# Expert slots in two halves: one weight tile converted in each half, the activation chain over two slots

## Chip, cores and metric

One core of a Trainium2 chip. The metric is the device time of one execution in microseconds (us); several executions are timed and their median is used, and one execution is recorded by the hardware profiler. Engines are named as in the profile: PE (TensorE, with its weight loads PEld), DVE (VectorE), ACT (ScalarE), POOL (GpSimd) and SP (the engine that issues most of the loads and stores).

## What is computed

A retention layer (linear attention with a decaying state), followed by two expert layers, all in float32. With B = 4, H = 8, S = 768, D = 64 there are 3072 tokens of width 512; each expert layer goes from 512 to 2048 and back.

```
state = gamma * state + k_t v_t^T          # per batch and head, t = 0 .. 767
y_t   = (1/sqrt(D)) * q_t state
x = y as 3072 x 512
x = (h - tanh(h)) @ w_out    with h = x @ w_in        # first expert layer
x = elu(h) @ w2_out          with h = x @ w2_in       # second expert layer
```

## The kernel before

**Tiling.** Tokens are worked on in six blocks of 512 (`NB` = 6). The retention is done in chunks of 128 positions: step s is chunk s // 4 of batch s % 4, so four steps make one block of tokens. The steps of block 0 (s = 0 to 3) are done at the start, the other twenty one at a time inside the expert layers, in the slots 1 to 20.

**Slots.** The expert layers run in two phases (`ph` 0 and 1, one for each layer), each over six blocks, each over 16 tiles `f` of 128 hidden units: 192 slots, numbered `n`. In slot n, PE makes `h` of this slot (`first_mm`, L267: twelve 128 x 512 matmuls) and adds the product of slot n - 2 into the four accumulators (`second_mm`, L334: twelve more; `SKEW` = 2). Weights and activations are each split into a high and a low part, and three products of the parts stand for one float32 product.

**Weights.** They arrive as 64-bit numbers. `convert_a` (ACT, L81), `convert_b` (three DVE instructions, L89, L93, L97) and `convert_c` (ACT, L109, the high part, and L112, the low part, on DVE or POOL) make a tile pair of one raw tile; the raw tile, the 32-bit tile `w32` and the result are in SBUF. In phase 0, block 0, two tiles are converted in a slot, in slots 0 to 12, after six at the start; the weights of phase 1 are converted in the last block of phase 0 and the first of phase 1, mostly one in a slot.

**Activation chain.** From `h` (in PSUM) ACT makes `u`, `v`, `t` and a mask `m`, and DVE runs four instructions: L293 (`v` and `u`, both in SBUF), L296 (`v` and `h`), L299 (`h` and `t`) and L300 (copies `h` into `v` where `m` says so, and is the last reader of `h`). There are two `h` buffers. One slot later `split_hi` (ACT, L276) and `split_lo` (L280, POOL in the blocks marked `busy`, DVE elsewhere) split `v` into `g`. In phase 1 the chain has two instructions (L313, L316).

**Retention in a slot.** PE makes the scores (L163) into PSUM, DVE masks them (L175, one instruction over 1024 columns), PE makes the output from the state (L202) and from the masked scores (L210) and the new state part (L189); DVE scales the output (`out_scale`, L221) and adds the state part (L244), and POOL multiplies the state by its decay (L245). POOL also scales the next step's `v` by `vtab` (L143), and in four slots of a block it makes the low part of the next block's x (L365).

**Order.** `manual_schedule` keeps the order in which the code is written, engine by engine. Each engine works through its queue in that order and waits where an operand or a buffer is not ready. In a slot of block 0 DVE's queue is: mask, two operations of `side` (both L89), scaling, state sum, and then `chain` and the rest of `side` in turn:

```
if s is not None:
    for op in side[:2]:
        op()
    side = side[2:]
    out_scale(s)
    state_add(s)
interleave(chain, side)
```

Of the kernel before, what the change touches and what calls it, by code (L numbers as in the profile page):

```python
# [36 lines left out]
def retention_moe_kernel(ctx: ExitStack, tc: tile.TileContext, dims, ins, out):  # L37
# [15 lines left out]
    stg = ctx.enter_context(tc.tile_pool(name="stg", bufs=4))  # L53
# [49 lines left out]
    def convert_c(job, engine):  # L103
# [5 lines left out]
        nc.scalar.activation(out=t[:, 0, :], in_=w, func=AF.Copy)  # L109

        def low():
            engine.tensor_tensor(  # L112
                out=t[:, 1, :], in0=w, in1=t[:, 0, :].bitcast(F32), op=ALU.subtract
            )

        if engine is nc.gpsimd:
            low()
            return []
        return [low]
# [16 lines left out]
    def load_v(s):  # L136
        v = v_t[s] = att.tile([P, TB], F32, tag="v", bufs=B, name=f"v{s}")
        nc.sync.dma_start(out=v, in_=ins["qkv"][s][:, 2, :])
# [12 lines left out]
    def att_psum(s):  # L151

        tag = ("a", "acc0", "acc1")[s % 3] if s < B else "a"
        return (ps_a if tag == "a" else ps_acc).tile([P, 2, TB], F32, tag=tag, name=f"ps{s}")

    def scores_pe(s):
        t = qk_t[s]
        ps = ps_t[s] = att_psum(s)
        sc = ps.rearrange("p j (a i) -> p j a i", a=NP)
        for p in range(NP):  # L160
            for j in range(2):
                r = slice(j * D, (j + 1) * D)
                nc.tensor.matmul(  # L163
                    out=sc[:, j, p, :],
                    lhsT=t[r, 1, p * P:(p + 1) * P],
                    rhs=t[r, 0, p * P:(p + 1) * P],
                    start=True, stop=True,
                )

    def scores_mask(s):  # L170
        if s < B:
            pt = tmp.tile([P, 2 * NP, P], F32, tag="g", bufs=G_BUFS, name=f"pt{s}")
        else:
            pt = att1.tile([P, 2 * NP, P], F32, tag="pt", name=f"pt{s}")
        nc.vector.tensor_tensor(  # L175
            out=pt,
            in0=ps_t[s].rearrange("p j (a i) -> p (j a) i", a=NP),
            in1=mask.to_broadcast([P, 2 * NP, P]),
            op=ALU.mult,
        )  # L180
        pt_t[s] = pt

    def states_mm(ds, s):
        v, kn = v_t.pop(s), kn_t.pop(s)
        for p in range(NP):
            for j in range(2):
                r = slice(j * D, (j + 1) * D)
                h = 2 * p + j
                nc.tensor.matmul(  # L189
                    out=ds[r, p, :], lhsT=kn[:, h * D:(h + 1) * D], rhs=v[:, h * D:(h + 1) * D],  # L190
                    start=True, stop=True,
                )

    def out_pe(s):
        t, v, pt = qk_t.pop(s), v_t[s], pt_t.pop(s)
        o = ps_t[s][:, 0, :].rearrange("p (a i) -> p a i", a=NP)
# [9 lines left out]
        for p in range(NP):  # L206
            for j in range(2):
                r = slice(j * D, (j + 1) * D)
                h = 2 * p + j
                nc.tensor.matmul(  # L210
                    out=o[r, p, :], lhsT=v[:, h * D:(h + 1) * D], rhs=pt[:, j * NP + p, :],
                    start=(b == 0), stop=True, skip_group_check=True,
                )
        if b and b < NCH - 1:
            states_mm(ps_t[s][:, 1, 0:NP * D].rearrange("p (a d) -> p a d", a=NP), s)

    def out_scale(s):

        xo = xo_t[s] = att.tile([P, NP, P], F32, tag="xo", bufs=3, name=f"xo{s}")
        o = ps_t[s][:, 0, :].rearrange("p (a i) -> p a i", a=NP)  # L220
        nc.vector.tensor_tensor(out=xo, in0=o, in1=qtab, op=ALU.mult)  # L221
# [17 lines left out]
    def state_add(s):  # L239
# [3 lines left out]
        ds = ps_t[s][:, 1, 0:NP * D].rearrange("p (a d) -> p a d", a=NP)  # L243
        nc.vector.tensor_tensor(out=st[:, c], in0=ds, in1=st[:, c], op=ALU.add)  # L244
# [4 lines left out]
    def first_states():  # L249
        ds = ps_a.tile([P, B, NP, D], F32, tag="a", name="ds")  # L250
        for c in range(B):
            states_mm(ds[:, c], c)
        for c in range(B):
            nc.vector.tensor_tensor(
                out=st[:, c], in0=ds[:, c], in1=gtab.to_broadcast([P, NP, D]), op=ALU.mult
            )
# [64 lines left out]
    def second_mm(m, f, n):  # L321
        g, w = g_t.pop(n), wts[m, f]
        if f == 0:
            for i in range(2):
                t = ps_acc.tile([P, 2, TB], F32, tag=f"acc{i}", name=f"acc{n}_{i}")
                acc[2 * i], acc[2 * i + 1] = t[:, 0, :], t[:, 1, :]
# [46 lines left out]
    with tc.manual_schedule():  # L373
# [9 lines left out]
        def interleave_into(dst, lists):  # L383
            while any(lists):
                for ops in lists:
                    if ops:
                        dst.append(ops.pop(0))

        def interleave(*lists):
            while any(lists):  # L390
                for ops in lists:
                    if ops:
                        ops.pop(0)()

# [4 lines left out]
        AHEAD = 6  # L399
# [6 lines left out]
        for s in range(B):  # L406
            load_qk(s, stage[:, s])
            load_v(s)
            fetch(*jobs0[s])
# [3 lines left out]
        for job in jobs0[B:AHEAD]:  # L413
            fetch(*job)
        load_qk(B, att.tile([P, 2, TB], F32, tag="qk", name=f"qk{B}"))
        for job in jobs0[AHEAD:AHEAD + 4]:
            fetch(*job)

        def conv(*ids):
            ops = []  # L420
            interleave_into(ops, [convert_b(jobs0[i]) for i in ids])
            for op in ops:
                op()

        def conv_low(*ids):
            for i in ids:
                for op in convert_c(jobs0[i], nc.vector if i % 2 else nc.gpsimd):
                    op()
# [3 lines left out]
        for s in range(2):  # L432
            scale_v(s, nc.gpsimd)
        warm(3)
# [6 lines left out]
        conv(0)  # L441
        out_scale(0)
        scores_pe(2)
        out_pe(1)
        for s in range(2, B):
            scale_v(s, nc.gpsimd)
        conv(1)
        out_split(0)
        scores_mask(2)
        out_scale(1)  # L450
        conv_low(0, 1)
        convert_a(jobs0[2])
        convert_a(jobs0[3])
        scores_pe(3)
        out_pe(2)
        conv(2)
        out_split(1)
        scores_mask(3)
        out_scale(2)
        conv(3)  # L460
        out_pe(3)
        conv_low(2, 3)
        convert_a(jobs0[4])
        convert_a(jobs0[5])
        out_split(2)
        out_scale(3)
        out_split(3)
        first_states()
        conv(4, 5)
        conv_low(4, 5)  # L470
# [3 lines left out]
        rest = jobs0[AHEAD:]  # L474
        for f in range(NF):
            todo[f] = rest[:2]
            rest = rest[2:]
        assert not rest
        base = (NB - 1) * NF
        for f in range(NF):  # L480
            todo[base + f + 2] = [(2, f)]
        for f in range(NF):
            todo.setdefault(base + (8 + 5 * f if f < 2 else NF + f - 1), []).append((3, f))
# [5 lines left out]
        prev_jobs = []  # L489
        for job in todo[0]:  # L490
            convert_a(job)
        prev_v = None

        def flush():
            if prev_v is not None:
                g_t[n - 1] = split_hi(prev_v, n - 1)
                if lo_engine is nc.gpsimd:
                    split_lo(g_t[n - 1], prev_v, nc.gpsimd)
# [9 lines left out]

        n = 0
        for ph in range(2):  # L510
            for b in range(NB):
                for f in range(NF):
                    first, last = b == 0, b == NB - 1
                    if ph == 0 and first:
                        for job in jobs0[AHEAD + 4 + 2 * f:AHEAD + 6 + 2 * f]:
                            fetch(*job)
                    jobs = todo.get(n, [])
# [3 lines left out]
                    s = step_of.get(n)  # L521
# [15 lines left out]
                    if s is not None:  # L537
                        for op in side[:2]:
                            op()
                        side = side[2:]  # L540
                        out_scale(s)
                        state_add(s)
                    interleave(chain, side)
                    for job in todo.get(n + 1, []):
                        convert_a(job)
                    prev_v = v
                    prev_jobs = jobs
# [3 lines left out]
                    second(SKEW)  # L551

# [8 lines left out]
                    if s is not None:  # L561
                        out_store(s)
# [7 lines left out]
        flush()  # L570
# [59 lines left out]
```

## Time and profile before

| | us |
|---|---|
| median of 3 runs | 1224.04 (1222.66 to 1224.7) |
| time of the profiled execution | 1222.74 |
| its span, first to last instruction | 1221.0 |
| PE busy | 1158.8 (95%) |
| DVE busy | 709.9 (58%) |
| ACT busy | 623.1 (51%) |
| POOL busy | 244.7 (20%) |

How to read it: the shares are means over stages that differ. In the 40 slices of the page DVE shows 6 to 8 tenths over the first eight slices and 9 from the 22nd to the 26th, while PE shows 9 in nearly all slices after the ninth. The granted clock is the share of full speed that TensorE was given; its mean over the run is 0.978.

### The profile page before, as it was taken

What the parts mean: (1) busy time and instruction counts of PE and PEld (TensorE: products, weight loads), DVE (VectorE), ACT (ScalarE), POOL (GpSimd) and SP (SyncE); (2) the same over time, 40 slices, a digit from 0 to 9 for tenths busy, and PEclk for the clock granted to TensorE, in tenths of its full rate; (3) what the DMA queues carried; (4) which work ended last, traced back from release to release, by engine and by line L of the source; (5) the groups of instructions that cost most, each with busy time, mean ns of one, the idle gap of its engine ahead of it and who ended that gap; (6) DMA issues with size and microseconds to landing.
All of it is one profiled execution on the core that took longest, in us unless ns stands there. A gap on an engine that the chain in (4) does not pass through costs nothing.

```text
span 1221.0 us, 15860 instructions
## 1 busy us (share of the span) xinstructions
PE 1158.8 (95%) x6030; PEld 950.1 (78%) x6030; DVE 709.9 (58%) x1004; ACT 623.1 (51%) x1089; POOL 244.7 (20%) x183
## 2 busy tenths in 40 slices
PE   5688889799999999999998999999999999999998
PEld 3576767578888888888887788888888888888886
DVE  6778886455655656556599999535334334343332
ACT  2344443225565565556677766544444544544443
POOL 2243543200001001001057557201001010010000
PEclk7889999999999999999999999999999999999999
DMA  9457554421010010010176410100100100100000
GB/s 360 158 184 227 190 161 130 130 64 32 1 61 9 1 61 9 1 61 10 66 217 200 141 59 9 60 2 9 61 10 1 61 9 1 61 9 1 35 1 35
DMA packets 41581, 88.40 MB, mean 72 GB/s; under 512 B 3872, under 2 KB 14240, under 8 KB 41504
## 3 DMA queue, kind: packets, MB, share of 16 engines
q1 hardware_dynamic: 40928, 87.05, 21.9%
q8 instruction: 47, 0.77, 0.3%
q10 hardware_dynamic: 576, 0.33, 0.1%
q14 instruction: 30, 0.25, 0.1%
HBM read 69.54 MB, written 17.83 MB: 72 GB/s over the span
## 4 chain that ended last, share of the span: by engine, by line
PE 75%; DVE 2%; issue 1%; ACT 1%; DMA 0%; SPq 0%; ACTq 0%; DVEq 0%
PE h L267 37%; PE acc L334 37%; DVE w L93 1%; DMA qk<-qkv 0%; DVE v L300 0%; DVE w L97 0%; DVE v L293 0%; PE ps L163 0%; DVE h L299 0%; PE ps L210 0%; PE ps L202 0%; DVE v L296 0%; ACT t L290 0%; ACT g L276 0%; DVE w L89 0%
## 5 line engine op out<-in xcount | busy, mean ns | idle before, releaser
L267 PE MATMUL h<-x,w 128*128 128x512 f32 x2304 | 558.8, 391 | 5.5 <-DVE v L300 5.5
L267 PEld LDWEIGHTS h<-x,w 128*128 128x128 f32 x2304 | 432.2, 188 | 98.6 <-DVE v L300 6.8
L334 PE MATMUL acc<-g,w 128*128 128x512 f32 x1152 | 280.3, 392 | 0.0
L334 PE MATMUL acc<-w,g 128*128 128x512 f32 x1152 | 276.7, 389 | 0.6 <-DVE g L280 0.6
L334 PEld LDWEIGHTS acc<-w,g 128*128 128x128 f32 x1152 | 216.1, 188 | 45.9 <-DVE g L280 1.0
L334 PEld LDWEIGHTS acc<-g,w 128*128 128x128 f32 x1152 | 215.6, 189 | 46.1 <-ACT g L276 0.7
L313 DVE SCALAR_TENSOR_TENSOR v<-v,t 128x512 f32<-128x512 f32 x96 | 77.1, 803 | 274.3 <-ACT t L311 274.1
L308 ACT ACTIVATE u<-h 128x512 f32<-128x512 f32 x96 | 57.5, 599 | 252.4 <-PE h L267 252.0
L365 POOL TENSOR_TENSOR x<-xin,x 128x512 fp32r<-128x512 f32 x44 | 60.2, 1368 | 617.8 <-ACT x L364 617.8
L287 ACT ACTIVATE u<-h 128x512 f32<-128x512 f32 x96 | 57.3, 597 | 208.0 <-issue 153.0
L293 DVE SCALAR_TENSOR_TENSOR v<-v,u 128x512 f32<-128x512 f32 x96 | 73.2, 762 | 134.9 <-ACT v L288 134.9
L280 DVE TENSOR_TENSOR g<-v,g 128x512 fp32r<-128x512 f32 x145 | 114.7, 791 | 21.2 <-ACT g L276 21.2
L276 ACT ACTIVATE g<-v 128x512 fp32r<-128x512 f32 x192 | 118.2, 616 | 11.9 <-DVE v L300 9.7
L280 POOL TENSOR_TENSOR g<-v,g 128x512 fp32r<-128x512 f32 x47 | 66.2, 1409 | 154.4 <-ACT g L276 91.7
L81 ACT ACTIVATE w<-raw 128x512 f32<-128x512 f32 x64 | 41.8, 662 | 85.1 <-DVE w L112 65.4
L112 POOL TENSOR_TENSOR w<-w,w 128x512 fp32r<-128x512 f32 x48 | 73.6, 1535 | 24.3 <-ACT w L109 24.3
L300 DVE COPY_PREDICATED v<-m,h 128x512 f32<-128x512 uint16 x96 | 70.6, 736 | 7.0
L288 ACT ACTIVATE v<-u,qa_b 128x512 f32<-128x512 f32 x96 | 69.5, 724 | 4.3
L291 ACT ACTIVATE m<-u,xs_b 128x512 bf16<-128x512 f32 x96 | 68.1, 710 | 0.0
L296 DVE SCALAR_TENSOR_TENSOR v<-v,h 128x512 f32<-128x512 f32 x96 | 65.3, 680 | 2.6 <-ACT t L290 1.9
L299 DVE TENSOR_TENSOR h<-h,t 128x512 f32<-128x512 f32 x96 | 66.2, 690 | 0.0
L316 DVE TENSOR_TENSOR v<-h,v 128x512 f32<-128x512 f32 x96 | 65.4, 681 | 0.0
(40 smaller groups left out, 742.5 us busy)
## 6 DMA issues: line engine op xcount, KB each, us to landing
raw<-w SPq DMA_DIRECT2D x64, 512.0 KB, 4.6
qk<-qkv SPq DMA_DIRECT2D x20, 512.0 KB, 6.2
v<-qkv SPq DMA_DIRECT2D x24, 256.0 KB, 5.7
x1d<-o SPq DMA_DIRECT2D x12, 512.0 KB, 3.2
xin<-x1d SPq DMA_DIRECT2D x24, 256.0 KB, 5.0
kn<-qkv SPq DMA_DIRECT2D x20, 256.0 KB, 6.1
x0d<-xo SPq DMA_DIRECT2D x20, 256.0 KB, 2.6
xin<-x0d SPq DMA_DIRECT2D x20, 256.0 KB, 4.3
```

The lines of the kernel that those rows point to most:

```text
L112: engine.tensor_tensor(out=t[:, 1, :], in0=w, in1=t[:, 0, :].bitcast(F32), op=ALU.subtract)
L267: nc.tensor.matmul(out=h, lhsT=w[:, a, c * P:(c + 1) * P], rhs=x[:, b, c, :], start=(i == 0), stop=(i == 3 * KC - 1),)
L276: nc.scalar.activation(out=t[:, 0, :], in_=g, func=AF.Copy)
L280: engine.tensor_tensor(out=t[:, 1, :], in0=g, in1=t[:, 0, :].bitcast(F32), op=ALU.subtract)
L288: nc.scalar.activation(out=v, in_=u, func=AF.Square, bias=qa_b)
L291: nc.scalar.activation(out=big, in_=u, func=AF.Relu, bias=xs_b)
L293: lambda: nc.vector.scalar_tensor_tensor(out=v, in0=v, scalar=QB, in1=u, op0=ALU.add, op1=ALU.mult),
L299: lambda: nc.vector.tensor_tensor(out=h, in0=h, in1=th, op=ALU.subtract),
L300: lambda: nc.vector.copy_predicated(out=v, mask=big.bitcast(U16), data=h),
L313: lambda: nc.vector.scalar_tensor_tensor(out=v, in0=v, scalar=1.0, in1=th, op0=ALU.add, op1=ALU.mult),
L316: lambda: nc.vector.tensor_tensor(out=v, in0=h, in1=v, op=ALU.max),
L334: nc.tensor.matmul(out=acc[e], lhsT=lhsT, rhs=rhs, start=(f == 0 and i == 0), stop=(f == NF - 1 and i == 2),)
```

## The change

- Block 0 converts one weight tile in each half of a slot. `convert_c` is cut in two (`convert_c` for the high part, `convert_d` for the low), and `weights(i, first)` issues for half i: the high part (ACT) and low part of half i - 1's tile, `convert_b` of half i's, `convert_a` of half i + 1's. In block 0 the low part of the first half's tile goes to DVE, that of the second half's to POOL. Four tiles instead of six are converted at the start (`AHEAD`), 28 in the slots 0 to 13. `w32` has five buffers instead of four.
- In `busy` blocks the chain is cut in the middle: two instructions (phase 1: one) in its own slot, the rest at the head of the next slot, in turn with the weight operations of its first half. `split_hi` and `split_lo` of slot n - 1 are issued together, ahead of slot n's chain.
- Masks, scaling and state sum: the mask is two instructions of 512 columns into two tiles; the scores, the output and the state part have PSUM tiles of one bank each (tags a0, a1, acc0 to acc3). The mask is at the head of the slot's first half, scaling and state sum at its end, before the second half.
- The states of block 0 (`first_states`) move into slot 0, behind `first_mm`; stores of the retention's output (`out_store`) are issued one slot later; `v` has three buffers and one more in another tile; the loads at the start come in another order.

```diff
+    def convert_c(job):
         m, f = job
-        w = w32.pop(job)
         del raw[job]
         t = wts[job] = wp.tile([P, 2, TB], F32R, tag=f"w{m % 2}_{f}", name=f"w{m}_{f}")
+        nc.scalar.activation(out=t[:, 0, :], in_=w32[job], func=AF.Copy)
+
+    def convert_d(job, engine):
+        t = wts[job]
+        engine.tensor_tensor(
+            out=t[:, 1, :], in0=w32.pop(job), in1=t[:, 0, :].bitcast(F32), op=ALU.subtract
+        )
...
+        for j in range(2):
+            nc.vector.tensor_tensor(
+                out=pt[j], in0=ps_t[s][j], in1=mask.to_broadcast([P, NP, P]), op=ALU.mult
+            )
...
+        def weights(i, first):
+            ops = []
+            if i - 1 in todo:
+                job = todo[i - 1]
+                convert_c(job)
+                if first and i % 2:
+                    ops.append(lambda: convert_d(job, nc.vector))
+                else:
+                    convert_d(job, nc.gpsimd)
+            if i in todo:
+                ops = convert_b(todo[i]) + ops
+            if i + 1 in todo:
+                convert_a(todo[i + 1])
+            return ops
...
                     h = first_mm(2 * ph, xhl[ph * NB + b], f, n)
+                    if n == 0:
+                        for g in ds:
+                            next(g)
+                    ops = weights(2 * n, early)
+                    while chain or ops:
+                        if chain:
+                            chain.pop(0)()
+                        if ops:
+                            ops.pop(0)()
                     if s is not None:
                         out_pe(s)
-                    v, chain = (act_elu if ph else act_tanhshrink)(h, n, flush)
-                    low = []
-                    for i, job in enumerate(prev_jobs):
-                        low += convert_c(job, nc.vector if first and not ph and i else nc.gpsimd)
-                    side = []
-                    interleave_into(side, [convert_b(j) for j in jobs])
-                    side += low
-                    if prev_v is not None and lo_engine is nc.vector:
-                        side.insert(0, lambda: split_lo(g_t[n - 1], prev_v, nc.vector))
-                    if s is not None:
-                        for op in side[:2]:
-                            op()
-                        side = side[2:]
                         out_scale(s)
                         state_add(s)
-                    interleave(chain, side)
-                    for job in todo.get(n + 1, []):
-                        convert_a(job)
+                    def flush():
+                        if prev_v is not None:
+                            g_t[n - 1] = split_hi(prev_v, n - 1)
+                            split_lo(g_t[n - 1], prev_v, lo_engine)
+                    v, chain = (act_elu if ph else act_tanhshrink)(h, n, flush)
+                    for op in weights(2 * n + 1, early):
+                        op()
+                    cut = len(chain) // 2 if busy else len(chain)
+                    for op in chain[:cut]:
+                        op()
+                    chain = chain[cut:]
                     prev_v = v
```

Three places in the order of the queues. First DVE in a slot of block 0 (slot 3): before, from behind the mask to the last instruction of the chain (`pt` is the masked scores, `xo` the scaled output, `w_0_7` and `w_1_5` the 32-bit tiles of the two weights, `v` and `h` the chain's).

```order
L89 TENSOR_SCALAR w_0_7_580<-w_0_7_580 128x512
L89 TENSOR_SCALAR w_1_5_582<-w_1_5_582 128x512
L221 TENSOR_TENSOR xo_676<-ps_610,qtab 128x512
L244 TENSOR_TENSOR st<-ps_610,st 128x256
L293 SCALAR_TENSOR_TENSOR v_660<-v_660,u_658 128x512
L93 SCALAR_TENSOR_TENSOR w_0_7_580<-raw_7_402,w_0_7_580 128x512
L296 SCALAR_TENSOR_TENSOR v_660<-v_660,h_3_621 128x512
L93 SCALAR_TENSOR_TENSOR w_1_5_582<-raw_5_404,w_1_5_582 128x512
L299 TENSOR_TENSOR h_3_621<-h_3_621,t_659 128x512
L97 SCALAR_TENSOR_TENSOR w_0_7_580<-raw_7_402,w_0_7_580 128x512
L300 COPY_PREDICATED v_660<-m_661,h_3_621 128x512
L97 SCALAR_TENSOR_TENSOR w_1_5_582<-raw_5_404,w_1_5_582 128x512
```

And after, in the same slot, from the scaling on to the first half of slot 4 (the lines have moved by two to four: L178 is the mask, L223 the scaling, L245 the state sum, L296 to L303 the chain). Ahead of these rows stand two mask halves, the chain's second pair of slot 2 and the three weight instructions of the first half.

```order
L223 TENSOR_TENSOR xo_679<-o_653,qtab 128x512
L245 TENSOR_TENSOR st<-ds_670,st 128x256
L89 TENSOR_SCALAR w_1_4_646<-w_1_4_646 128x512
L93 SCALAR_TENSOR_TENSOR w_1_4_646<-raw_4_316,w_1_4_646 128x512
L97 SCALAR_TENSOR_TENSOR w_1_4_646<-raw_4_316,w_1_4_646 128x512
L112 TENSOR_TENSOR w_6_694<-w_0_6_580,w_6_694 128x512
L296 SCALAR_TENSOR_TENSOR v_685<-v_685,u_683 128x512
L299 SCALAR_TENSOR_TENSOR v_685<-v_685,h_3_630 128x512
L178 TENSOR_TENSOR pt_0_738<-ps_0_728,mask 128x512
L178 TENSOR_TENSOR pt_1_739<-ps_1_729,mask 128x512
L302 TENSOR_TENSOR h_3_630<-h_3_630,t_684 128x512
L89 TENSOR_SCALAR w_0_7_696<-w_0_7_696 128x512
```

Behind the scaling and the state sum there were chain and weights in turn; now five instructions that read SBUF alone follow one another.

Second, POOL around the same slot, before: the low part of g, the low part of the weights, the state's decay, the next v, and the next low part of g.

```order
L280 TENSOR_TENSOR g_664<-v_551,g_664 128x512
L112 TENSOR_TENSOR w_6_669<-w_0_6_485,w_6_669 128x512
L245 TENSOR_TENSOR st<-st,gtab 128x256
L143 TENSOR_TENSOR v_705<-v_705,vtab 128x512
L280 TENSOR_TENSOR g_771<-v_660,g_771 128x512
```

And after (L246 is the decay, L283 the low part of g, L141 the scaling of v):

```order
L112 TENSOR_TENSOR w_3_643<-w_1_3_530,w_3_643 128x512
L246 TENSOR_TENSOR st<-st,gtab 128x256
L283 TENSOR_TENSOR g_689<-v_569,g_689 128x512
L141 TENSOR_TENSOR v_716<-v_716,vtab 128x512
L112 TENSOR_TENSOR w_4_755<-w_1_4_646,w_4_755 128x512
```

The decay, which waits for DVE's state sum, now stands ahead of the low part of g.

Third, DVE at the start (L231 is the low part of a quarter of x), before:

```order
L175 TENSOR_TENSOR pt_194<-ps_169,mask 128x1024
L175 TENSOR_TENSOR pt_204<-ps_183,mask 128x1024
L89 TENSOR_SCALAR w_0_0_192<-w_0_0_192 128x512
L93 SCALAR_TENSOR_TENSOR w_0_0_192<-raw_0_120,w_0_0_192 128x512
L97 SCALAR_TENSOR_TENSOR w_0_0_192<-raw_0_120,w_0_0_192 128x512
L221 TENSOR_TENSOR xo_211<-ps_169,qtab 128x512
L89 TENSOR_SCALAR w_0_1_206<-w_0_1_206 128x512
L93 SCALAR_TENSOR_TENSOR w_0_1_206<-raw_1_125,w_0_1_206 128x512
L97 SCALAR_TENSOR_TENSOR w_0_1_206<-raw_1_125,w_0_1_206 128x512
L231 TENSOR_TENSOR x_235<-xo_211,x_235 128x4x128
L175 TENSOR_TENSOR pt_238<-ps_213,mask 128x1024
```

And after (L233 is the low part of x):

```order
L178 TENSOR_TENSOR pt_209<-ps_0_185,mask 128x512
L178 TENSOR_TENSOR pt_209<-ps_1_186,mask 128x512
L223 TENSOR_TENSOR xo_233<-o_200,qtab 128x512
L89 TENSOR_SCALAR w_0_0_195<-w_0_0_195 128x512
L93 SCALAR_TENSOR_TENSOR w_0_0_195<-raw_0_123,w_0_0_195 128x512
L97 SCALAR_TENSOR_TENSOR w_0_0_195<-raw_0_123,w_0_0_195 128x512
L223 TENSOR_TENSOR xo_240<-o_224,qtab 128x512
L178 TENSOR_TENSOR pt_242<-ps_0_214,mask 128x512
L178 TENSOR_TENSOR pt_242<-ps_1_215,mask 128x512
L233 TENSOR_TENSOR x_245<-xo_233,x_245 128x4x128
```

The second scaling (`xo_240`), which waits for PE's second output, moved ahead of the second weight tile.

## Rows read from the trace of the kernel before

**Rows 1.** The page: span; PE's busy time, share and instructions.

```profile
span 1221.0 us, 15860 instructions
...
PE 1158.8 (95%) x6030; PEld 950.1 (78%) x6030; DVE 709.9 (58%) x1004; ACT 623.1 (51%) x1089; POOL 244.7 (20%) x183
```

**Rows 2.** Busy time by stretch: length; PE, PEld, DVE, ACT, POOL; clock, DMA share, GB/s.

```profile
83.67:95.86 12.19, 10.92 (x88) 9.06 (x88) 8.92 (x15) 5.21 (x9) 4.93 (x4) 0.86 0.58 187
95.86:107.35 11.49, 9.79 (x89) 7.59 (x88) 9.48 (x15) 5.21 (x9) 5.05 (x4) 1.00 0.69 221
...
179.32:191.20 11.88, 9.59 (x88) 7.59 (x88) 10.96 (x15) 5.89 (x11) 6.37 (x5) 1.00 0.39 113
198.00:207.50 9.50, 9.50 (x89) 7.59 (x88) 5.13 (x8) 2.93 (x5) 3.63 (x4) 1.00 0.48 154
```

**Rows 3.** Timeline of PE in block 0: start, length, instruction, [idle before <- releaser].

```profile
73.46 1.09 PE L202 MATMUL ps<-qk,st 64*64 64x128 f32 x16 [1.14 <-DVE pt L175]
74.48 1.09 PE L210 MATMUL ps<-pt,v 128*64 128x128 f32 x16
75.40 0.64 PE L189 MATMUL ps<-v,kn 128*64 128x64 f32 x16
...
84.94 1.09 PE L202 MATMUL ps<-qk,st 64*64 64x128 f32 x16 [1.92 <-DVE pt L175]
85.96 1.97 PE L210 MATMUL ps<-pt,v 128*64 128x128 f32 x16
...
192.59 1.09 PE L202 MATMUL ps<-qk,st 64*64 64x128 f32 x16 [2.41 <-DVE pt L175]
...
202.08 1.09 PE L202 MATMUL ps<-qk,st 64*64 64x128 f32 x16
...
243.44 2.08 PE L163 MATMUL ps<-qk 64*128 64x128 f32 x16 [7.80 <-DMA qk<-qkv]
```

**Rows 4.** Timeline of DVE in slot 5.

```profile
95.86 1.22 DVE L175 TENSOR_TENSOR pt<-ps,mask 128x1024 f32<-128x1024 f32 x1
...
99.76 0.69 DVE L221 TENSOR_TENSOR xo<-ps,qtab 128x512 f32<-128x512 f32 x1 [2.01 <-PE ps L189]
100.36 0.41 DVE L244 TENSOR_TENSOR st<-ps,st 128x256 f32<-128x256 f32 x1
100.69 1.25 DVE L293 SCALAR_TENSOR_TENSOR v<-v,u 128x512 f32<-128x512 f32 x1
101.86 1.10 DVE L93 SCALAR_TENSOR_TENSOR w<-raw,w 128x512 uint32<-128x512 uint32 x1
102.89 0.67 DVE L296 SCALAR_TENSOR_TENSOR v<-v,h 128x512 f32<-128x512 f32 x1
103.48 0.93 DVE L93 SCALAR_TENSOR_TENSOR w<-raw,w 128x512 uint32<-128x512 uint32 x1
```

**Rows 5.** Timeline of POOL in slot 5; of DVE and POOL at 670 us.

```profile
100.09 1.30 POOL L112 TENSOR_TENSOR w<-w,w 128x512 fp32r<-128x512 f32 x1 [0.28 <-ACT w L109]
101.35 1.06 POOL L245 TENSOR_TENSOR st<-st,gtab 128x256 f32<-128x256 f32 x1
102.38 1.49 POOL L143 TENSOR_TENSOR v<-v,vtab 128x512 f32<-128x512 f32 x1
...
670.48 0.85 DVE L93 SCALAR_TENSOR_TENSOR w<-raw,w 128x512 uint32<-128x512 uint32 x1
671.05 1.45 POOL L112 TENSOR_TENSOR w<-w,w 128x512 fp32r<-128x512 f32 x1 [0.26 <-ACT w L109]
```

**Rows 6.** Timeline: PE's second output at the start; DVE's mask of slot 1.

```profile
16.23 1.81 PE L210 MATMUL ps<-pt,v 128*64 128x128 f32 x16
...
47.64 1.22 DVE L175 TENSOR_TENSOR pt<-ps,mask 128x1024 f32<-128x1024 f32 x1
```

**Rows 7.** Who waited for whom, PE, 600 to 700 us: total, times, longest.

```profile
PE h L267 <- DVE v L300: 5.5, 3, 2.8
```

**Rows 8.** Timeline of PE: its last wait.

```profile
1211.26 5.32 PE L334 MATMUL acc<-w,g 128*128 128x512 f32 x22 [0.61 <-DVE g L280]
```

More of the change, by code (lines that the diff above doesn't have):

```diff
@@ L149, in load_kn @@
         kn_t[s] = kn
-    def att_psum(s):
-        tag = ("a", "acc0", "acc1")[s % 3] if s < B else "a"
-        return (ps_a if tag == "a" else ps_acc).tile([P, 2, TB], F32, tag=tag, name=f"ps{s}")
     def scores_pe(s):
+        pool, tags = ps_a, ("a0", "a1")
+        if s in (1, 2):
+            pool, tags = ps_acc, (f"acc{2 * s - 2}", f"acc{2 * s - 1}")
         t = qk_t[s]
-        ps = ps_t[s] = att_psum(s)
-        sc = ps.rearrange("p j (a i) -> p j a i", a=NP)
+        ps = ps_t[s] = [
+            pool.tile([P, NP, P], F32, tag=tags[j], name=f"ps{s}_{j}") for j in range(2)
+        ]
         for p in range(NP):
@@ L171, in scores_mask @@
         if s < B:
-            pt = tmp.tile([P, 2 * NP, P], F32, tag="g", bufs=G_BUFS, name=f"pt{s}")
-        else:
[L174 to L181, printed above, removed]
+            whole = tmp.tile([P, 2, NP, P], F32, tag="g", bufs=G_BUFS, name=f"pt{s}")
+            pt = pt_t[s] = [whole[:, j] for j in range(2)]
+        else:
+            pt = pt_t[s] = [
+                att1.tile([P, NP, P], F32, tag=f"pt{j}", name=f"pt{s}_{j}") for j in range(2)
+            ]
+        for j in range(2):
+            nc.vector.tensor_tensor(
+                out=pt[j], in0=ps_t[s][j], in1=mask.to_broadcast([P, NP, P]), op=ALU.mult
+            )
     def states_mm(ds, s):
-        v, kn = v_t.pop(s), kn_t.pop(s)
+        v, kn = v_t[s], kn_t[s]
         for p in range(NP):
@@ L247, in state_add, with first_states @@
         )
[L249 to L253, printed above, removed]
+    def first_states(i):
+        ds = ps_a.tile([P, 2, NP, D], F32, tag=f"a{i}", name=f"ds{i}")
+        for c in range(2):
+            states_mm(ds[:, c], 2 * i + c)
+        yield
+        for c in range(2):
             nc.vector.tensor_tensor(
-                out=st[:, c], in0=ds[:, c], in1=gtab.to_broadcast([P, NP, D]), op=ALU.mult
+                out=st[:, 2 * i + c], in0=ds[:, c], in1=gtab.to_broadcast([P, NP, D]), op=ALU.mult
             )
@@ L323, in second_mm @@
         if f == 0:
-            for i in range(2):
-                t = ps_acc.tile([P, 2, TB], F32, tag=f"acc{i}", name=f"acc{n}_{i}")
-                acc[2 * i], acc[2 * i + 1] = t[:, 0, :], t[:, 1, :]
+            for e in range(4):
+                acc[e] = ps_acc.tile([P, TB], F32, tag=f"acc{e}", name=f"acc{n}_{e}")
         for e in range(4):
@@ L408, in retention_moe_kernel @@
             load_v(s)
-            fetch(*jobs0[s])
+            if s % 2:
+                fetch(*jobs0[s - 1])
+                fetch(*jobs0[s])
+        for job in jobs0[B:B + 2]:
+            fetch(*job)
         kn23 = att.tile([P, 2, TB], F32, tag="qk", name="kn23")
@@ L507, in second @@
                     finish(pm, pb)
+        def weights(i, first):
[5 more added lines that the diff above has]
+                    ops.append(lambda: convert_d(job, nc.vector))
+                else:
+                    convert_d(job, nc.gpsimd)
[4 more added lines that the diff above has]
+            return ops
+        convert_a(todo[0])
+        chain = []
+        prev_v = None
+        ds = [first_states(i) for i in range(2)]
         n = 0
@@ L513, in retention_moe_kernel @@
                     first, last = b == 0, b == NB - 1
[L514 to L517, printed above, removed]
+                    early = ph == 0 and first
                     busy = (ph == 0 and (first or last)) or (ph == 1 and first)
@@ L569, in retention_moe_kernel @@
                     n += 1
-        flush()
+        for op in chain:
+            op()
+        g_t[n - 1] = split_hi(prev_v, n - 1)
         split_lo(g_t[n - 1], prev_v, nc.vector)
```

137 lines of the change are left out of this document (53 added, 84 removed).

## Prediction

> **What bounds the kernel now.** The page comes first: of a span of 1221.0 us TensorE is busy in 95% [rows 1], so only stretches in which PE waits can give anything. The busy time by stretch finds three: everything up to about 236 us (start and block 0), the last block of phase 0 (640 to 690 us), and the end. Between them PE is busy without a gap and the change touches nothing that it waits for.
>
> Block 0 is read slot by slot, from one mask (L175) to the next. The twelve stretches from 47.64 [rows 6] to 191.20 take 143.6 us, 11.96 a slot; a slot without weights, 198.0 to 207.5, takes 9.50 and is PE work throughout [rows 2]. So PE's own bound is 9.5, and weights cost 2.5 us a slot. DVE is not full there either: 8.9 to 9.5 us of 11.5 to 12.2 [rows 2]. The order of its queue is the reason. It does the mask and two L89, then sits until PE has made the output: L221 comes 3.90 us after the mask, 2.01 of it idle [rows 4]. PE meanwhile waits for that mask, 1.14 us in one slot and 1.92 in the next; after the 1.92 its L210 took 1.97 instead of 1.09, and the slot has a mean granted clock of 0.86 instead of 1.00 [rows 2, 3]. That makes the long slots.
>
> **The lock between VectorE and GpSimd.** On DVE's rows beside POOL's [rows 4, 5] one sees more than a slowdown. POOL's L245 starts at 101.35 but ends 0.47 after L293 (101.94), though the next DVE instruction, L93, started before L293's end. L93 ends at 102.96, 0.55 after L245 (102.41). POOL's L143 ends 0.91 after that (103.87), and the next L93 0.54 later (104.41). L296, which reads PSUM, takes 0.67 in the middle of L143. So an instruction with both inputs in SBUF and a POOL instruction alternate, first come first served, whole instruction by whole instruction; those with a PSUM input are free. Later in the run L93 ends at 671.33 and POOL's L112, started at 671.05, ends 1.17 after it [rows 5]: that is L112's hold, and I take it for L280 too, which reads the same shapes.
>
> The Trainium skill has this as a rule (SBUF — State Buffer, "Who interferes with whom"): the pair of ports that DVE's second SBUF input shares with GpSimd is an exclusive lock. The rows agree. By the rule a changed slot would be the 12.0 us worked out below; if the engines merely shared bandwidth it would be the 10.65 of rival 1.
>
> **A weighted slot after the change.** Counted from its first mask half; steps are start to start, 0.60 for 512 columns, 0.33 for L244 [rows 4] and for an L89 with something independent behind it (an estimate: both write in about that time), 0.73 where the next instruction needs this one (an estimate: the whole 0.68 of such an instruction and 0.05).
> - First half: two mask halves 1.20, L299 0.60, L89 0.33, L300 0.62, L93 0.73, L97 0.61: the output's scaling can start at 4.09. PE may start its output after the first mask half (about 0.75) and needs 2.6 (73.46 to 76.04 [rows 3]), so it is done by 3.3: the 2 us wait is gone. That is the change's gain. With scaling and state sum (0.94) DVE stands at 5.03. POOL has nothing to do in this half.
> - Second half: now come five DVE instructions with SBUF inputs alone (L89, L93, L97, L112, L293), and just here all four of POOL's become ready: the state's decay after the sum, then behind it in POOL's order the low part of g, the next v, and the low part of this half's weights. Alternating: L89 ends 5.43, POOL decay 5.91, L93 6.46, POOL g 7.63, L97 8.18, POOL v 9.09, L112 9.64, POOL weights 10.81, L293 11.36, and L296 clears the queue at **12.00**. Before, the low part of g ran in DVE's idle stretch, and that of the weights, from 100.09 [rows 5], mostly beside PSUM work.
>
> So the wait for PE turns into waits for POOL: 12.0 against 11.96. PE's work ends at 10.3, so it idles 2.45 us a slot. Idle of 1.9 and more was followed by the lower clock level (1.2 of 2.4 GHz) in four of six slots (84.94 the first, 192.59 the last, which itself stayed warm), of up to 1.4 in none of five (1.14 the first) [rows 3]. The lower level delays the output by about 1.4, of which 0.8 is covered here: 0.65 lost. As such a slot shortens the next wait, I take five of 13: 3.3 us, and 0.6 for the first slot that PE bounds again.
>
> **Start.** PE's second output ends at 18.04 (16.23 + 1.81) [rows 6], as before: the loads ahead of it carry the same bytes. DVE no longer fills that wait with a second weight tile. From 18.05 to the mask of slot 1 its queue holds fourteen instructions of 0.60 (three scalings, four mask halves, four x splits, three low parts), five tiles of 1.79, four state instructions of 0.33 and two of the chain: 20.0 us. Waits are an estimate, 6.2: three for ScalarE's x (0.7 to 1.5 each), one behind POOL, one for ScalarE's first pass, and 2 for the states on a PE that has just idled. So this mask stands at 44.2 (42.5 to 46), against 47.64 [rows 6]. But 28 instead of 26 tiles are left, so 13 weighted slots follow where 12 did: slot 14's output starts at 44.2 + 13 x 12.0 + 0.75 + 3.9 = 204.9, against 202.08 [rows 3]: **+2.8**. Everything behind runs at PE's pace as before, the 7.80 us wait for a load ahead of 243.44 [rows 3] too.
>
> **Last block of phase 0.** PE waits there for L300 three times, 5.5 us together [rows 7], in the slots with two tiles or an x split. Spread over two slots, the chain frees h about as late as before (6.2 us after h is ready, by the same alternation), because L300 now stands behind an L89 that waits for ScalarE's next pass. A second tile still costs its 1.8 us, and where an x split adds a fifth hold of 1.17, L293 and L89 each wait for one. Followed by hand this gives 6 to 7 us: **+1**, 3 either way.
>
> **End.** The last but one low part (L280) moves ahead of the chain, so PE's 0.61 wait for it [rows 8] goes: **-0.6**. Split masks and PSUM tags cost 0.07 a slot, in the sum above; stores a slot later are issued as soon as their data is ready, at nothing, since the loads do not stand behind them any more.
>
> **Sum:** 2.8 + 1 - 0.6 = +3.2. The profiled execution took 1222.74, the median of the runs is 1224.04, so I expect 1225.9 to 1227.2: **1226**. About 0.2%, 2.4 us, is what a measurement of this kernel can tell.
>
> **Rivals.**
> 1. *No alternation, faster.* POOL's last hold comes too late and L293 goes first: the margin is 0.5 us (9.05 against 9.56), and the hold would then lie beside masks, which are free. Slot 10.85. Or the collisions cost only what they cost on average before, about 0.4 us for each of POOL's 5: 8.75 + 1.9 = 10.65. Thirteen slots save 15 to 18, and PE, idling 1.2, stays warm: 1204 to 1212. The ends in rows 4 and 5 speak against it. 0.22.
> 2. *PE-bound, faster.* POOL falls wholly into the first half; slots of 9.6 to 9.9: 1193 to 1199. Its order (decay first, which needs the sum) forbids it. 0.04.
> 3. *The clock, slower.* If PE's 2.45 us of idle bring the lower level in every slot and the output comes late each time by 1.4 to 2, a slot is 12.65 to 13.2 and block 0 adds 5 to 12 more: 1230 to 1238. It decides from a slot of 12.2 upward. For it: the long slots of now. Against it: a cold slot shortens the next wait. 0.18.
> 4. *Forecast,* slots of 11.8 to 12.4, 1218 to 1231. 0.56, of which about 0.09 under 1221.6, 0.24 within 2.4 us of the median, 0.23 above.
>
> So faster 0.33, same 0.26, slower 0.41. The range has to reach into rival 1 and into rival 3: 1209 to 1236; the forecast's own is 1218 to 1231.
>
> **What would show it.** Right: no idle of DVE before the scaling in block 0; DVE busy over 95% there; L93, L97, L112 and L293 of the second half at 1.1 us and more, each ending 0.55 after a POOL end; slots of 12.0 to 12.6; PE idle over 2 us before L202; the first block-0 mask of slot 1 near 44; PE's waits for L300 after 640 us of 5 to 7. Wrong: slots under 11.3, L293 ending ahead of POOL's weights, or DVE still waiting for PE in most slots; any gap of PE between blocks 1 and 4 would be outside the argument altogether.

## The result, and the profile after

| | time, us | against the kernel before |
|---|---|---|
| before | 1223.79, median (1221.28 to 1224.7) | |
| after | 1231.85, median (1230.41 to 1237.08) | 1.0079, 95% interval 1.0056 to 1.0102 |

The change costs 0.8% by the ratio, which compares the means of the runs, and 0.7% by the medians. The profiled execution took 1232.28 us, with a span of 1230.5 against 1221.0 [rows 1]; 9.5 us have to be found. The page first (span; busy time, share and instructions of an engine; and the stores of the outputs, with the median time until they land, 5.1 us where it was 2.6 before):

```profile
span 1230.5 us, 15696 instructions
...
PE 1165.9 (95%) x6029; PEld 953.5 (77%) x6029; DVE 735.6 (60%) x1028; ACT 625.1 (51%) x1089; POOL 252.0 (20%) x183
...
x0d<-xo SPq DMA_DIRECT2D x20, 256.0 KB, 5.1
```

Then block 0 by slots, from mask (now L178) to mask, with the columns of [rows 2]:

```profile
91.77:103.66 11.89, 9.56 (x88) 7.59 (x88) 11.75 (x16) 5.85 (x10) 5.54 (x4) 1.00 0.67 215
103.66:115.58 11.92, 11.13 (x88) 8.99 (x88) 11.78 (x16) 4.82 (x9) 5.58 (x4) 0.86 0.37 125
115.58:127.48 11.90, 9.57 (x88) 7.59 (x88) 11.76 (x17) 5.86 (x10) 5.54 (x4) 1.00 0.67 216
127.48:139.41 11.93, 11.17 (x88) 8.94 (x88) 11.79 (x17) 5.32 (x10) 6.78 (x5) 0.86 0.01 4
139.41:156.88 17.47, 11.56 (x88) 9.18 (x88) 11.86 (x17) 6.36 (x11) 7.24 (x6) 0.90 0.45 150
156.88:174.86 17.98, 12.61 (x88) 10.07 (x88) 11.84 (x17) 5.31 (x10) 7.21 (x6) 0.81 0.72 233
```

VectorE is busy from end to end of an ordinary slot, which takes 11.9 us whether PE's granted clock is 1.00 or 0.86. But slot 9 takes 17.47, slot 10 takes 17.98, and VectorE worked no more in them. The timeline of SP, POOL and DVE at that place shows who waits (SPq rows are DMA issues):

```profile
120.36 0.53 SPq L239 DMA_DIRECT2D x0d<-xo  x1
...
131.54 0.68 DVE L223 TENSOR_TENSOR xo<-o,qtab 128x512 f32<-128x512 f32 x1
...
136.47 1.74 POOL L367 TENSOR_TENSOR x<-xin,x 128x512 fp32r<-128x512 f32 x1
...
138.24 0.33 SPq L362 DMA_DIRECT2D xin<-x0d  x1
138.62 0.90 SPq L77 DMA_DIRECT2D raw<-w  x2
139.56 0.43 SPq L136 DMA_DIRECT2D v<-qkv  x1
140.09 0.60 SPq L146 DMA_DIRECT2D kn<-qkv  x1
140.74 0.65 SPq L128 DMA_DIRECT2D qk<-qkv  x1
141.48 0.53 SPq L239 DMA_DIRECT2D x0d<-xo  x1
...
149.04 0.69 DVE L223 TENSOR_TENSOR xo<-o,qtab 128x512 f32<-128x512 f32 x1 [5.47 <-DMA x0d<-xo]
```

Slot 8's output is scaled by 132.22. Its store now stands on SP behind the x load (L362) of slot 8's end, and that load needs the buffer that POOL's x split (L367) gives back at 138.21. So SP stands from about 121 to 138.24, issues the x load and five more, and then the store, at 141.48. Two of the three xo buffers hold x loads, so slot 9's scaling needs this one back and starts at 149.04. Slot 10 repeats it (wait 6.00, at 167.03). The chain of work that ended last runs through both stores:

```profile
141.29 0.19 DVE w L89
141.48 7.46 DMA x0d<-xo
...
158.95 7.99 DMA x0d<-xo
```

Elsewhere the slot is the one that was forecast. The timeline of DVE and POOL in the second half of slot 5:

```profile
95.84 0.68 DVE L223 TENSOR_TENSOR xo<-o,qtab 128x512 f32<-128x512 f32 x1
...
96.94 0.72 POOL L246 TENSOR_TENSOR st<-st,gtab 128x256 f32<-128x256 f32 x1 [6.36 <-ACT w L108]
97.23 0.98 DVE L93 SCALAR_TENSOR_TENSOR w<-raw,w 128x512 uint32<-128x512 uint32 x1
97.63 1.71 POOL L283 TENSOR_TENSOR g<-v,g 128x512 fp32r<-128x512 f32 x1
98.25 1.64 DVE L97 SCALAR_TENSOR_TENSOR w<-raw,w 128x512 uint32<-128x512 uint32 x1
99.30 1.49 POOL L141 TENSOR_TENSOR v<-v,vtab 128x512 f32<-128x512 f32 x1
99.81 1.53 DVE L112 TENSOR_TENSOR w<-w,w 128x512 fp32r<-128x512 f32 x1
100.75 1.73 POOL L112 TENSOR_TENSOR w<-w,w 128x512 fp32r<-128x512 f32 x1
101.26 1.77 DVE L296 SCALAR_TENSOR_TENSOR v<-v,u 128x512 f32<-128x512 f32 x1
```

Ends alternate: POOL 97.66, DVE 98.21, POOL 99.34, DVE 99.89, POOL 100.79, DVE 101.34, POOL 102.48, DVE 103.03. Each DVE end is 0.55 behind a POOL end.

### The profile page after: what moved, and what is told of

The parts are those of the page before. It is cut to its first block, busy times and chain, and to the rows that moved or that the text cites. A ratio compares the mean times of both kernels' runs of the same rounds, so it can differ in the third digit from the quotient of the medians.

```text
span 1230.5 us, 15696 instructions
## 1 busy us (share of the span) xinstructions
PE 1165.9 (95%) x6029; PEld 953.5 (77%) x6029; DVE 735.6 (60%) x1028; ACT 625.1 (51%) x1089; POOL 252.0 (20%) x183
## 4 chain that ended last, share of the span: by engine, by line
PE 79%; DVE 16%; DMA 3%; issue 2%; ACT 0%; SPq 0%; DVEq 0%; ACTq 0%
PE acc L336 38%; PE h L270 38%; DVE v L296 3%; DVE w L97 3%; DVE w L93 2%; DVE w L112 2%; DVE pt L178 1%; DMA x0d<-xo 1%; DVE v L299 1%; DVE v L303 1%; PE o L210 1%; DVE h L302 1%; DVE w L89 1%; PE o L202 1%; PE ps L162 1%
## 5 line engine op out<-in xcount | busy, mean ns | idle before, releaser
L283 DVE TENSOR_TENSOR g<-v,g 128x512 fp32r<-128x512 f32 x145 | 100.3, 692 | 387.4 <-ACT g L279 387.4
L367 POOL TENSOR_TENSOR x<-xin,x 128x512 fp32r<-128x512 f32 x44 | 60.8, 1381 | 611.0 <-ACT x L366 611.0
L296 DVE SCALAR_TENSOR_TENSOR v<-v,u 128x512 f32<-128x512 f32 x96 | 89.1, 928 | 4.6 <-ACT v L291 4.6
L283 POOL TENSOR_TENSOR g<-v,g 128x512 fp32r<-128x512 f32 x47 | 73.2, 1558 | 84.6 <-issue 47.7
L112 POOL TENSOR_TENSOR w<-w,w 128x512 fp32r<-128x512 f32 x48 | 77.2, 1608 | 23.9 <-ACT w L108 21.9
L303 DVE COPY_PREDICATED v<-m,h 128x512 f32<-128x512 uint16 x96 | 70.6, 736 | 6.9
L108 ACT ACTIVATE w<-w 128x512 fp32r<-128x512 f32 x64 | 40.0, 625 | 62.0 <-DVE w L97 61.8
```

The costliest lines, as they stand in the source:

```text
L112: engine.tensor_tensor(out=t[:, 1, :], in0=w32.pop(job), in1=t[:, 0, :].bitcast(F32), op=ALU.subtract)
L283: engine.tensor_tensor(out=t[:, 1, :], in0=g, in1=t[:, 0, :].bitcast(F32), op=ALU.subtract)
L296: lambda: nc.vector.scalar_tensor_tensor(out=v, in0=v, scalar=QB, in1=u, op0=ALU.add, op1=ALU.mult),
L303: lambda: nc.vector.copy_predicated(out=v, mask=big.bitcast(U16), data=h),
```

## The experiments

Two questions: is it the queue with its ring of buffers that makes the two long slots, and is it POOL's place in the slot that makes the ordinary ones 11.9?

**1. store_own: the store back in its own slot.**

```diff
-                    if sp is not None:
-                        out_store(sp)
+                    if s is not None:
+                        out_store(s)
```

> The changed kernel, with each output stored in its own slot again, ahead of that slot's x load, and nothing else. Theory (the x load of slot 8 waits for POOL's x split, and the late store stands behind it in SP's queue, so the next scaling has no free buffer): VectorE's waits for a store (5.47 and 6.00 us at 149.04 and 167.03) go, every weighted slot takes 11.9 us, and the time falls by 11.5 to 1220 to 1222 us. Rival (the two buffers held by x loads are the cause, wherever the store stands, or the stores are slow because weights load beside them): the waits stay, 1230 to 1233 us.

Measured 1222.44 us (1216.8 to 1225.68), ratio 0.9988, interval 0.9975 to 1.0001. No wait for a store is left; slots of 11.89 to 12.27. The store of slot 8 is issued at 132.82, while the x load behind it still waits until 138.77. The waits went as the theory has it; the median fell by 9.4 us, a little less than the expected 11.5. What remains of the change does not differ from the kernel before by what can be measured.

**2. xo_bufs4: late stores, four buffers.**

```diff
-    stg = ctx.enter_context(tc.tile_pool(name="stg", bufs=5))
+    stg = ctx.enter_context(tc.tile_pool(name="stg", bufs=4))
...
-        xo = xo_t[s] = att.tile([P, NP, P], F32, tag="xo", bufs=3, name=f"xo{s}")
+        xo = xo_t[s] = att.tile([P, NP, P], F32, tag="xo", bufs=4, name=f"xo{s}")
```

(and the same number at the x loads)

> The changed kernel, its late stores kept, with four instead of three buffers for scaled outputs and x loads together (and four instead of five for the weights in conversion, to pay for it). No instruction moves on any engine. Theory: SP still waits about 18 us for POOL's x split and the store still lands near 149, but the scaling takes another buffer: no wait of VectorE for a store, 1220 to 1223 us. Rival (it is the queue or the transfers themselves, not the buffers): still two slots of over 17 us, 1230 us or more.

Measured 1221.86, ratio 0.9983 (0.9975 to 0.9992). The timeline, DVE and SP:

```profile
126.65 0.33 SPq L362 DMA_DIRECT2D xin<-x0d  x1
...
133.22 0.53 SPq L239 DMA_DIRECT2D x0d<-xo  x1
...
139.38 0.34 SPq L362 DMA_DIRECT2D xin<-x0d  x1
144.40 0.69 DVE L223 TENSOR_TENSOR xo<-o,qtab 128x512 f32<-128x512 f32 x1
```

The waits are gone, so the shortage of buffers is needed for the loss. One thing I had wrong: the fourth buffer also eases SP. The x load of slot 8 finds its buffer earlier (126.65, not 138.24), so the store behind it is issued at 133.22 and not at 141.48. The run separates buffers from transfers, but not buffers from queue; with store_own, removing either is enough.

**3. before_late: the late store alone, in the kernel before.**

```diff
-                    if s is not None:
-                        out_store(s)
+                    sp = step_of.get(n - 1)
+                    if sp is not None:
+                        out_store(sp)
```

> The kernel before, with each output stored a slot later, behind the x load of its own slot, and nothing else. Theory: two of the three buffers are held by x loads here too, and the x load of slot 8 waits for POOL's x split, which ends near 145; so the scalings of two slots wait for a store that lands 3 to 7 us after that: +6 to +14, 1230 to 1238 us. Rival (the late store hurts only together with the new order of the conversions): 1223 to 1225 us.

Measured 1241.33, ratio 1.0143 (1.0128 to 1.0158): +17.6, more than the expected 6 to 14, because the two waits are longer (10.78, shown here, and 9.97):

```profile
145.60 1.31 POOL L365 TENSOR_TENSOR x<-xin,x 128x512 fp32r<-128x512 f32 x1 [4.86 <-ACT x L364]
146.93 0.33 SPq L360 DMA_DIRECT2D xin<-x0d  x1
149.95 0.53 SPq L237 DMA_DIRECT2D x0d<-xo  x1
157.97 0.69 DVE L221 TENSOR_TENSOR xo<-ps,qtab 128x512 f32<-128x512 f32 x1 [10.78 <-DMA x0d<-xo]
```

The same chain: POOL's split, x load, store, scaling. The late store needs nothing else of the change to hurt.

**4. g_first and pool_order: POOL's order.** Both have store_own's store. g_first moves the call for POOL's decay behind the low part of g:

```diff
                             split_lo(g_t[n - 1], prev_v, lo_engine)
+                        if s is not None:
+                            state_decay(s)
```

> store_own with one swap: on POOL the low part of g stands ahead of the state's decay. Turn-taking, followed by hand: g asks for its turn at 3.55, behind L97, and holds 1.17 beside the scaling, the state sum and L89, which read PSUM or one SBUF tile; decay holds from 5.2 to 5.7, L93 to 6.25, v to 7.16, L97 to 7.7, L112 to 8.25; the weights' low part is ready only near 8.4, when L296 is already in line, and then lies beside the next masks. A slot of 9.5 to 10.2, the four with an x split 11.5 to 13: 1198 to 1206 us. If the weights' low part wins the tie against L296, slots of 10.7 to 11: 1207 to 1213. If the order on POOL mattered only through the place of v and the weights (the other half of pool_order), slots of 11.5 or more: 1217 to 1222.

pool_order has that and prepares v a slot sooner, so that POOL's order is weights, v, g, decay:

```diff
                     ops = weights(2 * n, early)
+                    nx = step_of.get(n + 1)
+                    if nx is not None:
+                        load_v(nx)
+                        scale_v(nx, nc.gpsimd)
...
-                        load_v(nx)
...
-                        scale_v(nx, nc.gpsimd)
```

> The changed kernel with each output stored in its own slot, and with another order of POOL's four instructions of a slot: the low part of the weights, the next v (loaded and scaled one slot sooner), the low part of g, and the state's decay last, where it was decay, g, v, weights. No instruction is added and none moves on VectorE or ScalarE. If instructions with two SBUF inputs and POOL's take turns (the forecast's term), POOL's long ones now lie beside masks and the chain's PSUM instructions, the second half is free but for the decay, and a slot falls from 11.9 to 9.5 to 10.2 us, where PE bounds it: 1189 to 1200 us. If both engines only share a bandwidth, or VectorE's own work bounds the slot, the order changes nothing: slots of 11.9, 1219 to 1223 us. If only the pressure behind the mask matters (POOL late, PE late), something between, slots of 10.7 to 11.2, 1205 to 1212 us.

Measured: g_first 1202.37, ratio 0.9817 (0.9804 to 0.9830), slots of 9.88 to 10.00 and four of 12.1 to 12.2; pool_order 1200.9, ratio 0.9815 (0.9803 to 0.9828), slots of 10.0 to 10.8, three of 12.2 to 13.0 and the last two of 9.2 and 9.4. One swap of two calls on an engine that is busy for 20% of the span takes 20 us off store_own. Each turn can be read in a slot of g_first (timeline, DVE and POOL):

```profile
98.32 0.69 DVE L97 SCALAR_TENSOR_TENSOR w<-raw,w 128x512 uint32<-128x512 uint32 x1
98.52 1.67 POOL L288 TENSOR_TENSOR g<-v,g 128x512 fp32r<-128x512 f32 x1 [3.15 <-issue]
98.93 0.69 DVE L223 TENSOR_TENSOR xo<-o,qtab 128x512 f32<-128x512 f32 x1
...
100.14 0.79 POOL L251 TENSOR_TENSOR st<-st,gtab 128x256 f32<-128x256 f32 x1
100.50 0.98 DVE L93 SCALAR_TENSOR_TENSOR w<-raw,w 128x512 uint32<-128x512 uint32 x1
100.89 1.49 POOL L141 TENSOR_TENSOR v<-v,vtab 128x512 f32<-128x512 f32 x1
101.51 1.41 DVE L97 SCALAR_TENSOR_TENSOR w<-raw,w 128x512 uint32<-128x512 uint32 x1
102.85 0.68 DVE L112 TENSOR_TENSOR w<-w,w 128x512 fp32r<-128x512 f32 x1
103.45 0.68 DVE L301 SCALAR_TENSOR_TENSOR v<-v,u 128x512 f32<-128x512 f32 x1
103.67 1.62 POOL L112 TENSOR_TENSOR w<-w,w 128x512 fp32r<-128x512 f32 x1 [1.29 <-ACT w L108]
```

POOL's g now holds beside the scaling, which reads PSUM and still takes 0.69; L112 and L301 (the chain's first step) take 0.68 where they took 1.53 and 1.77, and POOL's weights fall behind them. If VectorE's own work had bounded the slot, no order on POOL could have shortened it; that the two take whole turns, and do not share a bandwidth, rests on the ends listed above. pool_order came out a little above its range: in most slots v had not landed when its turn came and started only 3.4 to 4.4 us into the slot, so g held later.

**5. pool_early: v loaded earlier still, and the x split moved too.** The load of v is issued two slots ahead; POOL's half of the x split goes behind the next slot's weights and v, and the last two x loads go a slot later:

```diff
+    XLOAD, XSPLIT = (6, 7, 9, 10), (8, 9, 11, 12)
...
+                    if ph * NB + b + 1 < 2 * NB and f - 1 in XSPLIT:
+                        split_x_low(ph * NB + b + 1, XSPLIT.index(f - 1))
...
+                    if n + 2 in step_of:
+                        load_v(step_of[n + 2])
```

> pool_order, with v loaded another slot sooner, and the x split's low part put behind the next slot's weights and v on POOL (the last two x loads a slot later, so that SP doesn't block). Turn-taking: pool_order's slots of 10.0 to 10.8 came from a v that had not landed until 3.8 to 4.0 after the mask, so that g held past the scaling, and its three slots of 12.2 to 13.0 from an x split in the second half; both go, every weighted slot takes 9.5 to 10.0 us, and the time is 1190 to 1196 us. If PE's own work or VectorE's bounds the slot at 10 already, only the three long slots come down: 1193 to 1197. If something else made those slots long (the x loads, the weights' DMA), 1199 to 1202.

Measured 1188.11, ratio 0.9702 (0.9690 to 0.9715): 3.0% faster than the kernel before. The thirteen weighted slots of store_own, and of pool_early, each as one stretch:

```profile
44.34:199.82 155.48, 129.73 (x1132) 103.77 (x1132) 153.17 (x196) 70.59 (x120) 79.44 (x57) 0.95 0.56 185
```

```profile
44.98:168.69 123.71, 122.35 (x1131) 98.23 (x1132) 121.50 (x196) 69.23 (x119) 67.78 (x56) 0.99 0.70 226
```

The same 196 instructions of DVE are busy for 153.17 us in one and 121.50 in the other. A slot falls from 11.96 to 9.52, which is the slot without weights of the kernel before [rows 2]: PE bounds it, busy 122.35 of 123.71. The time is under the expected range by 2; of that the last block of phase 0 gives 1.5 (PE waits 4.2 there for the chain, not 5.7 as in pool_order). That the x split's new place did this is likely, but was not tried by itself.

**6. last_whole and combined: the chain not spread in the last block of phase 0.**

```diff
-                    cut = len(chain) // 2 if busy else len(chain)
+                    cut = len(chain) // 2 if busy and not (ph == 0 and last) else len(chain)
```

last_whole is store_own with this line, combined is pool_early with it.

> store_own with the chain not spread over two slots in the last block of phase 0 (in block 0 it stays so). If spreading costs something there, as the forecast's +1 us has it, PE's waits for the chain's end (5.8 us in five waits) fall by 0.3 to 1 and the time is 1221 to 1222 us. If spreading helps there, the waits grow to 8 to 12 us and the time to 1224 to 1228. If it makes no difference, the same waits within 0.3 and the time of store_own.

> pool_early with the chain not spread in the last block of phase 0. If the two act in different places and add up, pool_early's waits for the chain's end (4.2 us in four waits) fall by about 2 and the time from 1188.1 to 1185 to 1187 us. If they share their gain (the x split's new place had already taken it), 1188 or more.

last_whole: 1219.87, ratio 0.9966 (0.9953 to 0.9978). PE's waits on VectorE in that block fall from 5.8 us (five) to 3.3 (four) and 0.3 (one), by 2.2, and the median by 2.6; the interval only just meets store_own's. By these waits, from one profile of each kernel, spreading costs there, as forecast, and some more than its share of the +1. combined: 1187.35, ratio 0.9707 (0.9694 to 0.9721), not to be told from pool_early; its waits are 3.5 against 4.2.

**7. before_pool: POOL's order in the kernel before.**

```diff
+                    if nx is not None:
+                        scale_v(nx, nc.gpsimd)
...
+                    if s is not None:
+                        state_decay(s)
```

(the first behind the low part of g, the second behind the weights; x loads and splits as in pool_early)

> The kernel before, with POOL's order of a slot changed in the same spirit as in pool_early: low part of g, the next v (loaded two slots ahead), the low part of the weights, the decay, where it was g, weights, decay, v; x loads and x splits as in pool_early. It asks what the halves themselves are worth once POOL stands well. If the halves are needed (without them VectorE still sits idle about 2 us for PE's output, and PE for the mask), v moves beside the scaling and the sum, the weights' part still meets L293, about 0.4 to 0.9 us a slot is saved: 1212 to 1219 us, 24 or more above pool_early. If POOL's order alone is what counts, and the halves nothing, 1186 to 1195. If the tie of L293 and the weights' part goes the wrong way, nothing is saved: 1221 to 1225.

Measured 1221.54, ratio 0.9982 (0.9972 to 0.9991). Some slots fall to 11.35, others take 12.4 to 12.9, and the twelve average 11.92, against 11.96. VectorE still waits there for PE's output:

```profile
112.65 0.69 DVE L221 TENSOR_TENSOR xo<-ps,qtab 128x512 f32<-128x512 f32 x1 [2.01 <-PE ps L189]
```

So the better order on POOL is worth 34 us with the halves (store_own to pool_early, the earlier loads of v included) and about 2 in the one form tried without them (1 to 3.4 by the interval); the halves with POOL's old order are worth about nothing. Whether another order would help the kernel before was not tried.

## Why the prediction was right in its slot, wrong in its sum and lucky in its sign

The time fell inside the range and on the slower side, but that is luck. The forecast's own range ended at 1231; 1231.85 lies in the part that was kept for rival 3, and the cause was none of the rivals. Without the late store (store_own) the ratio is 0.9988, with an interval that includes 1, and slot 14's output starts at 200.56, 1.5 us ahead of the 202.08 of before [rows 3]. So the slower side came from a term that the prediction had put at nothing.

**The step that failed** is "stores a slot later are issued as soon as their data is ready, at nothing, since the loads do not stand behind them any more". True of the loads that used to stand behind the store, but the store had moved behind another one: the previous slot's x load, which waits for POOL, while three buffers serve stores and x loads alike. Forecast 0, measured 5.47 + 6.00 = 11.5 us; store_own gave back 9.4 of the median, and before_late showed the late store alone to cost 17.6. The trace of before gave the warning: in block 0 its x loads are issued at once behind their store (slots 6 and 7) or 2.5 us later, when that store has landed (slots 8 and 9), so the two share buffers; and over the whole run nine x loads stand on SP waiting for POOL's split, 281 us together.

**The clock term was mis-sized: forecast 3.9 us (3.3 in the weighted slots, 0.6 in the first slot that PE bounds again), measured about 2.0 (0.5 and 1.5).** In the ordinary slots PE's wait is 0.74 to 0.79 us in one and 2.31 to 2.33 in the next. After 2.33 the lower of the two levels (1.2 GHz) does come, but late and into a gap (timeline of PE in slot 8):

```profile
128.22 1.09 PE L202 MATMUL o<-qk,st 64*64 64x128 f32 x16 [2.33 <-DVE pt L178]
129.24 1.59 PE L210 MATMUL o<-pt,v 128*64 128x128 f32 x16
130.60 1.07 PE L188 MATMUL ds<-v,kn 128*64 128x64 f32 x16
```

L210 ends at 130.83, 0.5 later than at full clock; the scaling is due at 131.54, because DVE still has a conversion ahead of it. I had put 1.4 of delay against 0.8 of cover. One weighted slot did pay, slot 12: there L202 itself is slow, and the scaling waits for PE (timeline of PE and DVE):

```profile
187.50 1.81 PE L202 MATMUL o<-qk,st 64*64 64x128 f32 x16 [2.32 <-DVE pt L178]
...
191.26 0.69 DVE L223 TENSOR_TENSOR xo<-o,qtab 128x512 f32<-128x512 f32 x1 [0.35 <-PE o L210]
```

That slot takes 12.36, about 0.5 more than the others. Rival 3 wanted 0.65 to 1.2 in every slot and falls. Slot 14, which has no weights, paid more: L202 there to the next is 11.02 us (211.76 to 222.78), 1.5 over the 9.50 of before.

**Right:** the turn-taking, and with it the slot: 12.00 forecast, 11.89 to 11.93 in most; rivals 1 and 2 fall with it. VectorE's idle time ahead of the scaling is gone but for the two store waits and the 0.35 in slot 12; PE's wait of over 2 us ahead of its output came in every second slot, not in each. The rule of the Trainium skill (SBUF — State Buffer, "Who interferes with whom") holds in this trace: a loser waits out the whole instruction, POOL holding 1.13, 0.90 and 1.14 us between the DVE ends above. The first mask: 44.2 forecast, 44.10, with two misses of about 0.9 that cancel: PE's second output ended at 17.08 (15.11 + 1.97), not at 18.04, and from its scaling to the mask it took 27.0 us, not 26.2. The end: the 0.61 wait [rows 8] is gone. The last block: +1 forecast, +0.3 measured (5.8 us in five waits against [rows 7]); last_whole shows two effects behind it, spreading at about +2.2 and the rest of the change at about -1.9.

**The sum.** Slot 14's output starts at 211.76, 6.9 behind the forecast 204.9: 11.5 for the stores, less 3.4 for the clock (0.5 by then, not 3.9), less about 1.1 for slots of 11.9 and the start. From [rows 3] that is +9.7; slot 14 adds 1.5, the load's wait takes 0.4 (7.40, not 7.80), the last block adds 0.3, the end takes 0.6: +10.5 against a span that grew by 9.5. Of the microsecond between them 0.7 lies behind PE's last matmul, which ends 3.7 us before the span does (1226.82 of 1230.5) where it was 4.4 (1216.58 of 1221.0); the reason is not shown. The chances were not added up exactly either: rivals 1 and 2 and the forecast's part under 1221.6 make 0.35 for faster, and 0.24 is left for same, where the prediction has 0.33 and 0.26.

## What to carry to other kernels

A DMA that is moved later in a queue has to be followed past each entry that it now stands behind, with what that entry waits for and which buffers the two share; here a store that "only" slipped one slot cost 9 to 11 us in this kernel and 18 in the other. Where VectorE and GpSimd both read SBUF, the order on the engine with time to spare decided the slot here: place its long instructions, by what releases them, beside VectorE's PSUM reads, before VectorE is given less to do. Splitting work finer made room for that order, and in the forms tried neither paid without the other.

## What the runs showed of the hardware that was not expected

L89 has one input, in SBUF, and g_first's expectation counted it as free of POOL (the prediction let it wait only in the last block of phase 0). It is not free. In pool_early it takes 1.25 us instead of 0.42 and ends 0.29 after POOL's x split (timeline, DVE and POOL):

```profile
120.91 1.28 POOL L376 TENSOR_TENSOR x<-xin,x 128x512 fp32r<-128x512 f32 x1
121.23 1.25 DVE L89 TENSOR_SCALAR w<-w 128x512 uint32<-128x512 uint32 x1
```

The trace of before had it already: at the start an L89 from 12.08 takes 1.04 us and ends 0.28 after POOL's L143, which runs from 11.80 to 12.84.

The Trainium skill has this case too (SBUF — State Buffer, "Who interferes with whom"): a tensor_scalar that runs in a two-port mode takes the shared pair. The 0.42 us of a 128x512 L89 beside the 0.68 of L93 fits such a mode; the runs show only the wait.

The two stores that leave SP right behind six loads (the x load, two raw tiles, v, kn and qk) land 7.46 and 7.99 us after their issue, where the median over the slots from 40 to 240 us is 2.8 in store_own and before; that the loads are the reason was not tried. It mattered only because a scaling needed the buffer.
